# One ring of seven PSUM banks and another order of matmuls in an attention kernel

## The chip, the cores and the metric

The kernel runs on one core of one Trainium2 chip. The core's engines work side by side and are tied by semaphores: TensorE (PE in the profile, its weight loads PEld), VectorE (DVE), ScalarE (ACT), GpSimd (POOL) and SyncE (SP, which here only issues DMAs). PE writes its results to PSUM, which has eight banks of 128 partitions by 512 float32; DVE and ACT read them from there. The metric is the device time of one execution in microseconds. Before the change the median of 3 runs is 2832.03 us (2831.45 to 2834.38).

## The reference

Two attentions over the same 2048 rows of 576 are mixed by a gate. Attention A has 32 heads of 18 with their own keys and values, attention B has 32 heads of queries over one shared key and value.

```python
x = A_x
g = sigmoid((x * gate_w).sum(-1, keepdims=True))
# A: q, k, v = split(x @ wqkv) into 32 heads; B: q = x @ wq in 32 heads, k = x @ wk, v = x @ wv shared
scores = einsum("bhqd,bhkd->bhqk", q, k) * 18 ** -0.5
o = einsum("bhqk,bhkd->bhqd", softmax(scores), v)      # then heads side by side, @ wo
return g * a + (1 - g) * b
```

All is float32. The queries and the shared key of B are drawn eight times as large, so the softmax needs the maximum of each row.

## The kernel before, in words

The 64 heads of both attentions (those of B first) run one behind the other, each as 16 steps of 128 keys (or, for the maxima, 128 queries). Projections are done first; queries and keys come back from DRAM into tiles `qs` and `ks` that hold everything twice, at partitions 0 (`SB`) and 64 (`MB`). A float32 value is kept as a high and a low part, three products stacked to 54 rows; two more rows hold ones on the side of the keys and the negated row maximum on the side of the queries, so that one matmul of 56 rows gives score minus maximum.

One step T of the main loop has three parts.

- Scores (`step_scores`): four matmuls (chunks of 512 queries), each into a PSUM bank, each followed by an exp on ACT into an SBUF tile `pt` (12 of them).
- Maxima (`step_max`), 22 steps (`LEAD`) ahead of the scores: four matmuls with the queries as weights, 512 keys each. DVE reduces each bank to a column. In every second step two of the four are taken together: one matmul computes the scores for the difference of two key chunks (`kd`), ACT takes the relu of it into `xb`, and DVE adds `xb` to the other chunk's scores and takes the maximum in one custom operation. A pair of steps has eight max matmuls, seven DVE operations and nine ACT operations.
- Sums (`step_pv`): the exps times the values, with a column of ones for the denominator, added up in the bank `acc` over the 16 steps of a head. Four matmuls, one for each chunk, stand side by side in four groups of 32 columns of PE. P takes step A of the pair before over all 512 columns, h0 and h1 take step B in halves of 256.

When a head's sums are complete, `head_out` copies `acc` to `oe` on ACT and sends it off. When a head's maxima are complete, `max_rows` reduces and transposes them on DVE, splits them on POOL, and sends them through DRAM into rows 54 and 55 of `qs` (two DMAs on SP; four for the last two heads). The output projection (`out_proj`) is cut into 96 units of one PSUM tile each, 12 matmuls of 288 columns for the first 64 (`pm`, L507) and 3 for the last 32. `due` spreads them: 32 over T = 521 to 857, 32 over T = 942 to 1008, the last from T = 1021.

The order of all engines is the order in which the Python emits them (`manual_schedule`); each engine runs its instructions in that order. Two steps A and B are emitted together from one string of names: s is scores, m maxima, the digit the chunk. A matmul on `SB` and one on `MB` that follow each other run at the same time on the two halves of PE's rows. PSUM: `ps_s` three banks for scores and projections, `ps_m` four for maxima, units and the small rest, `ps_o` the accumulator. A tile takes the banks of its pool in turn, and its first matmul waits until the bank's last readers are done.

Of the kernel before, what the change touches and what calls it, by code (L numbers as in the profile page):

```python
# [17 lines left out]
S = 2048  # L18
# [24 lines left out]
def gated_mix_kernel(ctx: ExitStack, tc: tile.TileContext, xT, wall, wv, wo, out):  # L43
# [97 lines left out]

    def project(mt, c, w):

        fp = ps_s.tile([P, 512], F32, name="ps")
# [12 lines left out]
        if c == 1 and mt in HAS_K:  # L157
            d = stp.tile([P, 512], F32, name="pd", bufs=1)
            nc.vector.tensor_tensor(d, fp, KD.pop(mt), op=OP.subtract)
            dh, dl = (stp.tile([P, 512], F32R, name=f"pd{y}", bufs=1) for y in "hl")  # L160
            split(d, dh, dl, nc.scalar, nc.vector)
        dma(qk_d[0][mt * P:(mt + 1) * P, cs], h, nc.scalar)
        dma(qk_d[1][mt * P:(mt + 1) * P, cs], l, nc.gpsimd)
        if c == 1 and mt in HAS_K:
            dma(kd_d[0][mt * P:(mt + 1) * P, :], dh, nc.scalar)
            dma(kd_d[1][mt * P:(mt + 1) * P, :], dl, nc.gpsimd)
        if mt == 0:
            dma(z_d[cs], st[ROW_G:ROW_G + 1, :], nc.scalar)
            return c, st

    def shared_v(c, st):
        pv = ps_m.tile([P, 512], F32, name="pm")
# [9 lines left out]
        nc.gpsimd.memset(t, 1.0)  # L182

    def project_v(st_, hf, w):
        fp = ps_s.tile([P, 512], F32, name="ps")
        for n, (a, b, k, kr) in enumerate(PROJ):
            nc.tensor.matmul(fp[:, 0:288], X[b][:kr, k, st_ * P:(st_ + 1) * P], w[a][:kr, k, :],  # L187
                             start=(n == 0), stop=(n == len(PROJ) - 1))
# [129 lines left out]
    def kst(u):  # L318
        return ksb if u < H else L["ks"][(u - H) % 3]
# [6 lines left out]

    MX = {}

    def step_max(u, i, c):

        if i == 0 and c == 0:
            MX[u] = mxs[u] if u < 2 else mxs[2 + u % 3]
        early = 16 * u + i < LEAD
        both = not early and i % 2 == 0
        b = SB if early and c % 2 else MB
        pm = ps_m.tile([P, 512], F32, name="pm")
        k = kst(u)[b:b + 54, c * 512:(c + 1) * 512]
        if both and c < 2:  # L340
            k = L["kd", u if u >= H else 0][b:b + 54, :] if c == 0 else kst(u)[b:b + 54, 0:512]
        nc.tensor.matmul(pm, qs[u % 3][b:b + 54, i * P:(i + 1) * P], k, start=True, stop=True)  # L342
        if both and c == 0:
            MX["x"] = lead.tile([P, 512], F32, name="xb", bufs=2)
            nc.scalar.activation(MX["x"], pm, AF.Relu)  # L345
        elif both and c == 1:
            junk = lead.tile([P, 512], BF16, name="junk", bufs=1)
            nc.vector.tensor_tensor_reduce(junk, pm, MX.pop("x"), 1.0, -3e38, op0=OP.add, op1=OP.max,  # L348
                                           accum_out=MX[u][:, i, c:c + 1])
        else:  # L350
            nc.vector.tensor_reduce(MX[u][:, i, c:c + 1], pm, axis=AX.X, op=OP.max)  # L351

    def max_rows(u):


        m = ms[u % 2]
        nc.vector.tensor_reduce(m[:, 0:16], MX.pop(u), axis=AX.X, op=OP.max, negate=True)
        mt = lead.tile([P, 32], F32, name="mt")
        nc.vector.transpose(mt, m)  # L359
        mh = lead.tile([P, 2, 32], F32R, name="mh")  # L360
        split(mt, mh[:, 0, :], mh[:, 1, :], nc.gpsimd, nc.gpsimd)
        md = m_d[u % 4]
        dma(md, mh.rearrange("p a f -> p (a f)"))
        for b in (SB, MB) if u > NU - 3 else (SB,):
            for a in range(2):
                dma(qs[u % 3][b + 54 + a:b + 55 + a, :].rearrange("o (i b f) -> o i b f", b=4, f=32),
                    md.rearrange("(b i) (o a f) -> o a i b f", i=32, o=1, a=2)[:, a, 0:16])

    PT = {}

    def step_scores(u, i, c, alone):

        b = SB
        ps = (ps_m if alone and c < 2 else ps_s).tile([P, 512], F32, name="pm" if alone and c < 2 else "ps")
        if alone and c % 2:
            b = MB
        nc.tensor.matmul(ps, kst(u)[b:b + 56, i * P:(i + 1) * P],  # L377
                         qs[u % 3][b:b + 56, c * 512:(c + 1) * 512], start=True, stop=True)
        PT["q"] = PT.get("q", []) + [(c, ps)]
        if alone and c == 0:  # L380
            return
        for c, ps in PT.pop("q"):
            pt = L["pt"].tile([P, 512], F32, name="pt")
            nc.scalar.activation(pt, ps, AF.Exp, scale=SCALE)  # L384
            PT[u, i, c] = pt

    def step_pv(u, i, a, b):

# [88 lines left out]
    def out_proj(t0, rows, first=False):  # L477
# [18 lines left out]
        for q in range(8):  # L496
# [3 lines left out]
            for s2 in range(2):  # L500
                st_ = 2 * q + s2
                for hf in range(2):
                    fp = ps_m.tile([P, 512], F32, name="pm")
                    n = 0
                    for a, b in PRODS:
                        for t, r in enumerate(rows):
# [27 lines left out]
    def last_out():  # L534
# [6 lines left out]
        for j in range(4):  # L541
# [4 lines left out]
        pt = ps_m.tile([P, 512], F32, name="pm")  # L546
# [7 lines left out]
        yield  # L554
        for st_ in range(16):
            for hf in range(2):
                ps = ps_m.tile([P, 512], F32, name="pm")
# [49 lines left out]

    vunits = [(st_, hf) for hf in range(2) for st_ in range(16)]

    for T in range(-LEAD, NSTEP + 2, 2):  # L610
        if T == 0:
            open_ph2()
# [5 lines left out]
        alone = M >= NSTEP  # L618
        units = sum(due(t, Tb, Tc, 32) for t in (T, T + 1) for _, _, _, Tb, Tc in SEG)
        for op in "sA0 mA0 P sA1 mA1 sA2 mA2 sA3 mA3 h0 sB0 mB0 sB1 mB1 h1 sB2 mB2 sB3 mB3".split():  # L620
            if op[0] == "m":
                if T < 0 and op[2] == "0":
                    while len(vunits) > 32 * (-T - 1 - (op[1] == "B")) // LEAD:
                        project_v(*vunits[0], WV[vunits[0][1]])
                        vunits.pop(0)
                if not alone:
                    step_max(*divmod(M + (op[1] == "B"), 16), int(op[2]))
            elif op[0] == "s":
                if 0 <= T < NSTEP:
                    step_scores(*divmod(T + (op[1] == "B"), 16), int(op[2]), alone)  # L630
# [4 lines left out]
            if op[0] == "h" and units:  # L635
                pull(1)
                units -= 1
        pull(units)
        if slow and M % 16:
            for _ in range(2 if T > 1000 else 1):  # L640
# [45 lines left out]
```

## Time and profile before

| | |
|---|---|
| median of 3 runs | 2832.03 us |
| profiled execution | 2830.23 us, span 2828.1 us, mean granted clock 0.996 |
| PE busy | 2801.4 us (99%) |
| ACT busy | 2447.0 us (87%) |
| DVE busy | 2371.8 us (84%) |
| exps, L384 | 4052 records, 613 ns mean |
| reductions, L351 | 3094 records, 681 ns mean |
| score matmuls, L377, and max matmuls, L342 | 433 to 435 ns and 439 to 471 ns mean |
| sums, L391 | 12288 records, 457 ns mean |
| copy of the sums, L401 | 63 records, 617 ns median |

Durations overlap: the next instruction of an engine starts before the one before it has ended, so the interval between two starts is the price, not the duration. Some records of instructions are missing. PE's busy time has modelled ends. A row of the order of time has the start, the length, the engine, the line, the operation, output and input tile, the count of like instructions that were merged, and in brackets the idle time before them with what ended it.

### The profile page before, as it was taken

To read this page: it belongs to the slowest core of one execution; us is meant where nothing else is said; L and a number is where in the kernel's file an instruction comes from. 1 tells how busy PE (TensorE), PEld (TensorE's weight loads), DVE (VectorE), ACT (ScalarE), POOL (GpSimd) and SP (SyncE) were. 2 spreads that over 40 slices of the span, in tenths; PEclk is the share of its full clock that TensorE was granted. 3 is DMA by queue.
4 is the path that set the end of the run, shared out by engine and by line. 5 is a ranking of instruction groups with operands and counts; after the bars stand their busy time and mean duration, and the time that the engine had idled before them with its cause. 6 is when DMAs were issued, how large, how long until landed. Compare 5 with 4: busy or idle time off the path is not lost.

```text
span 2828.1 us, 58626 instructions
## 1 busy us (share of the span) xinstructions
PE 2801.4 (99%) x22628; PEld 1289.3 (46%) x22628; DVE 2371.8 (84%) x4461; ACT 2447.0 (87%) x4832; POOL 207.6 (7%) x364
## 2 busy tenths in 40 slices
PE   7999999999999999999999999999999999999999
PEld 5888443343433433434434444444444444345554
DVE  3346999999999999999999888888888888998765
ACT  3331999999999999999999999999999999997775
POOL 2220000011001000100110001000100011011000
PEclk9999999999999999999999999999999999999998
DMA  8662011121112111211143233233232323243412
GB/s 251 236 222 71 25 29 32 32 57 46 38 26 60 45 32 34 70 40 30 44 107 92 69 84 94 60 84 82 73 84 75 80 68 86 59 104 97 101 35 91
DMA packets 137147, 215.16 MB, mean 76 GB/s; under 512 B 55437, under 2 KB 94301, under 8 KB 125182
## 3 DMA queue, kind: packets, MB, share of 16 engines
q1 hardware_dynamic: 116156, 168.13, 22.6%
q10 hardware_dynamic: 14120, 22.30, 2.2%
q0 software_dynamic: 6592, 20.99, 2.1%
q8 instruction: 178, 2.92, 0.4%
q14 instruction: 101, 0.83, 0.1%
HBM read 137.31 MB, written 64.77 MB: 71 GB/s over the span
## 4 chain that ended last, share of the span: by engine, by line
PE 95%; DMA 2%; DVE 1%; SPq 0%; issue 0%; ACT 0%; POOL 0%; DVEq 0%; ACTq 0%; POOLq 0%
PE ps L377 40%; PE acc L391 38%; PE pm L342 6%; PE ps L147 5%; PE pm L507 4%; PE ps L187 2%; DMA xs<-xT 1%; DVE oacc L561 0%; PE pm L377 0%; DMA ksb<-qkl 0%; SPq L49 0%; DVE oacc L515 0%; DMA qkh<-ph 0%; DMA vg<-v_d 0%; DMA qkl<-pl 0%; DMA ksa<-qkh 0%
## 5 line engine op out<-in xcount | busy, mean ns | idle before, releaser
L384 ACT ACTIVATE pt<-ps 128x512 f32<-128x512 f32 x4052 | 2111.6, 613 | 106.0 <-PE pm L342 37.5
L351 DVE TENSOR_REDUCE mx<-pm 128x1 f32<-128x512 f32 x3094 | 1902.0, 681 | 63.1 <-PE pm L342 53.7
L377 PE MATMUL ps<-qs,ksb 56*128 56x512 f32 x2688 | 905.3, 433 | 0.0
L342 PE MATMUL pm<-ksb,qs 54*128 54x512 f32 x2363 | 815.3, 440 | 0.2
L377 PEld LDWEIGHTS ps<-qs,ksb 56*128 56x128 f32 x2688 | 442.8, 184 | 657.5 <-ACT pt L384 628.8
L391 PE MATMUL acc<-pt,vg 128*19 128x256 f32 (+1 forms) x6144 | 591.3, 457 | 0.8 <-ACT oe L401 0.8
L391 PE MATMUL acc<-pt,vb 128*19 128x256 f32 (+1 forms) x6144 | 591.5, 457 | 0.0
L348 DVE CUSTOM_DVE_ANT_0 junk<-pm,xb 128x512 bf16<-128x512 f32 x501 | 345.9, 690 | 192.7 <-ACT xb L345 150.2
L377 PE MATMUL ps<-qs,ksa 56*128 56x512 f32 x1364 | 459.2, 435 | 0.0
L342 PE MATMUL pm<-ksa,qs 54*128 54x512 f32 x1232 | 431.1, 439 | 0.0
L342 PEld LDWEIGHTS pm<-ksb,qs 54*128 54x128 f32 x2363 | 377.4, 184 | 5.8 <-issue 3.4
L377 PEld LDWEIGHTS ps<-qs,ksa 56*128 56x128 f32 x1364 | 220.3, 184 | 318.9 <-ACT pt L384 295.4
L345 ACT ACTIVATE xb<-pm 128x512 f32<-128x512 f32 x501 | 312.7, 624 | 0.2 <-PE pm L342 0.2
L391 PEld LDWEIGHTS acc<-pt,vg 128*19 128x19 f32 x6144 | 104.3, 97 | 223.5 <-issue 214.5
L391 PEld LDWEIGHTS acc<-pt,vb 128*19 128x19 f32 x6144 | 104.2, 96 | 212.0 <-issue 204.7
L342 PEld LDWEIGHTS pm<-ksa,qs 54*128 54x128 f32 x1232 | 197.6, 184 | 0.2
L342 PE MATMUL pm<-kdb,qs 54*128 54x512 f32 x373 | 175.5, 471 | 0.4 <-DVE mx L351 0.3
L116 POOL CAST mh<-mt 128x32 fp32r<-128x32 f32 x64 | 13.5, 211 | 1723.8 <-DVE mt L359 1723.8
L150 ACT ACTIVATE ph<-ps 128x512 fp32r<-128x512 f32 x56 | 33.5, 597 | 99.6 <-PE ps L147 88.2
L156 DVE TENSOR_TENSOR pl<-ps,ph 128x512 fp32r<-128x512 f32 x56 | 38.5, 691 | 95.8 <-ACT ph L150 63.3
L147 PE MATMUL ps<-xh,wh 128*128 128x512 f32 x280 | 75.7, 401 | 18.9 <-ACT xh L210 13.7
L147 PE MATMUL ps<-xh,wl 128*128 128x512 f32 x280 | 73.4, 392 | 0.0
(99 smaller groups left out, 1346.6 us busy)
## 6 DMA issues: line engine op xcount, KB each, us to landing
qs<-qkh SPq DMA_DIRECT2D x244, 144.0 KB
qs<-qkl SPq DMA_DIRECT2D x122, 144.0 KB
qkh<-ph ACTq DMA_DIRECT2D x56, 256.0 KB
qkl<-pl POOLq DMA_DIRECT2D x56, 256.0 KB, 3.2
ksa<-qkh SPq DMA_DIRECT2D x88, 144.0 KB
onh<-oh SPq DMA_DIRECT2D x32, 256.0 KB
onl<-ol SPq DMA_DIRECT2D x32, 256.0 KB
oih<-onh SPq DMA_DIRECT2D x16, 512.0 KB
```

Source lines behind the costliest of these rows:

```text
L147: nc.tensor.matmul(fp, w[a][:kr, k, :], X[b][:kr, k, cs], start=(n == 0), stop=(n == len(PROJ) - 1))
L150: nc.scalar.activation(h, fp, AF.Copy)
L156: nc.vector.tensor_tensor(l, fp, h.bitcast(F32), op=OP.subtract)
L187: nc.tensor.matmul(fp[:, 0:288], X[b][:kr, k, st_ * P:(st_ + 1) * P], w[a][:kr, k, :], start=(n == 0), stop=(n == len(PROJ) - 1))
L342: nc.tensor.matmul(pm, qs[u % 3][b:b + 54, i * P:(i + 1) * P], k, start=True, stop=True)
L345: nc.scalar.activation(MX["x"], pm, AF.Relu)
L348: nc.vector.tensor_tensor_reduce(junk, pm, MX.pop("x"), 1.0, -3e38, op0=OP.add, op1=OP.max, accum_out=MX[u][:, i, c:c + 1])
L351: nc.vector.tensor_reduce(MX[u][:, i, c:c + 1], pm, axis=AX.X, op=OP.max)
L377: nc.tensor.matmul(ps, kst(u)[b:b + 56, i * P:(i + 1) * P], qs[u % 3][b:b + 56, c * 512:(c + 1) * 512], start=True, stop=True)
L384: nc.scalar.activation(pt, ps, AF.Exp, scale=SCALE)
L391: nc.tensor.matmul(acc[32 * j:32 * j + 19, a:b], v_of(u, i), PT[u, i, j][:, a:b], start=(i == 0), stop=(i == 15), skip_group_check=True)
L507: nc.tensor.matmul(fp[:, 0:288], o[b][:r, t, s2 * P:(s2 + 1) * P], w[a][:r, t, 288 * hf:288 * hf + 288], start=(n == 0), stop=(n == 3 * nt ...
```

## The change

One pool `ring` of seven banks takes the place of `ps_s` and `ps_m`; every tile for scores, maxima, projections and units takes its banks in turn, in the order of emission. Four strings give the order: for the lead, for pairs without a unit, for pairs with a unit, and for the last pairs, which have no maxima. A capital M or S puts the matmul on the other half of the partitions than a small letter (maxima `SB`, scores `MB`). P stays; h and H are the halves of step B's sums; Q is step B's sums over 512 columns, and U pulls a unit. In pairs with a unit, three groups of sums become two, P and Q, and the unit stands between matmuls for scores and maxima. The combined maxima move from step A to step B (`mBx` is the difference and its relu, `mB0` the custom operation). The copy of the head's sums follows H or Q at the pair's end. The row maxima go to both halves of `qs` for every head, so four DMAs instead of two. In the last pairs each score matmul is followed by its own exp, and up to four units are pulled.

```diff
-    ps_s = ctx.enter_context(tc.tile_pool(name="ps_s", bufs=3, space=PSUM))
-    ps_m = ctx.enter_context(tc.tile_pool(name="ps_m", bufs=4, space=PSUM))
+    ring = ctx.enter_context(tc.tile_pool(name="ring", bufs=7, space=PSUM))
...
-    def step_max(u, i, c):
+    def step_max(u, i, c, low=False):
...
-        early = 16 * u + i < LEAD
-        both = not early and i % 2 == 0
-        b = SB if early and c % 2 else MB
-        pm = ps_m.tile([P, 512], F32, name="pm")
-        k = kst(u)[b:b + 54, c * 512:(c + 1) * 512]
-        if both and c < 2:
-            k = L["kd", u if u >= H else 0][b:b + 54, :] if c == 0 else kst(u)[b:b + 54, 0:512]
+        both = 16 * u + i >= LEAD and i % 2 == 1
+        b = SB if low else MB
+        if c == "x":
+            k = L["kd", u if u >= H else 0][b:b + 54, :]
+        else:
+            k = kst(u)[b:b + 54, c * 512:(c + 1) * 512]
+        pm = ring.tile([P, 512], F32, name="ps")
         nc.tensor.matmul(pm, qs[u % 3][b:b + 54, i * P:(i + 1) * P], k, start=True, stop=True)
-        if both and c == 0:
+        if c == "x":
             MX["x"] = lead.tile([P, 512], F32, name="xb", bufs=2)
             nc.scalar.activation(MX["x"], pm, AF.Relu)
-        elif both and c == 1:
+        elif both and c == 0:
...
-        for b in (SB, MB) if u > NU - 3 else (SB,):
+        for b in (SB, MB):
...
-    def step_scores(u, i, c, alone):
-        b = SB
-        ps = (ps_m if alone and c < 2 else ps_s).tile([P, 512], F32, name="pm" if alone and c < 2 else "ps")
-        if alone and c % 2:
-            b = MB
+    def step_scores(u, i, c, b):
+        ps = ring.tile([P, 512], F32, name="ps")
         nc.tensor.matmul(ps, kst(u)[b:b + 56, i * P:(i + 1) * P],
                          qs[u % 3][b:b + 56, c * 512:(c + 1) * 512], start=True, stop=True)
-        PT["q"] = PT.get("q", []) + [(c, ps)]
-        if alone and c == 0:
-            return
-        for c, ps in PT.pop("q"):
-            pt = L["pt"].tile([P, 512], F32, name="pt")
-            nc.scalar.activation(pt, ps, AF.Exp, scale=SCALE)
-            PT[u, i, c] = pt
+        pt = L["pt"].tile([P, 512], F32, name="pt")
+        nc.scalar.activation(pt, ps, AF.Exp, scale=SCALE)
+        PT[u, i, c] = pt
...
+    PLAIN = "mA0 sA0 sA1 mA1 sA2 mA2 P mA3 sA3 sB0 mB2 MB3 mBx h sB1 mB0 sB2 SB3 H"
+    UNIT = "mA0 sA0 sA1 mA1 sA2 mA2 P mA3 sA3 sB0 SB1 sB2 mB2 U MB3 mBx sB3 mB0 Q"
+    ALONE = "sA0 SA1 P U sA2 SA3 U sB0 SB1 h U sB2 SB3 H U"
+    LEADS = "V mA0 MA1 mA2 MA3 V.B mB0 MB1 mB2 MB3"
...
-        for op in "sA0 mA0 P sA1 mA1 sA2 mA2 sA3 mA3 h0 sB0 mB0 sB1 mB1 h1 sB2 mB2 sB3 mB3".split():
...
+        for op in (LEADS if T < 0 else ALONE if M >= NSTEP else UNIT if units else PLAIN).split():
+            k, second, c = op[0], op[1:2] == "B", op[2:]
+            c = int(c) if c.isdigit() else c
...
+            elif k in "mM":
+                step_max(*divmod(M + second, 16), c, k == "M")
+            elif k in "sS":
+                if T < NSTEP:
+                    step_scores(*divmod(T + second, 16), c, MB if k == "S" else SB)
+            elif k == "U":
+                pull(min(units, 1))
+                units -= min(units, 1)
             elif T >= 2:
-                step_pv(*divmod(T - (2 if op == "P" else 1), 16), *{"P": (0, 512), "h0": (0, 256), "h1": (256, 512)}[op])
-                if op == "h1" and T % 16 == 0 and T < NSTEP:
+                step_pv(*divmod(T - (2 if k == "P" else 1), 16), 256 * (k == "H"), 256 if k == "h" else 512)
+                if k in "HQ" and T % 16 == 0 and T < NSTEP:
                     head_out(T // 16 - 1)
```

More of the change, by code (lines that the diff above doesn't have):

```diff
@@ L142, in project @@
     def project(mt, c, w):
-        fp = ps_s.tile([P, 512], F32, name="ps")
+        fp = ring.tile([P, 512], F32, name="ps")
         cs = slice(c * 512, (c + 1) * 512)
@@ L171, in shared_v @@
     def shared_v(c, st):
-        pv = ps_m.tile([P, 512], F32, name="pm")
+        pv = ring.tile([P, 512], F32, name="ps")
         for j in range(4):
@@ L184, in project_v @@
     def project_v(st_, hf, w):
-        fp = ps_s.tile([P, 512], F32, name="ps")
+        fp = ring.tile([P, 512], F32, name="ps")
         for n, (a, b, k, kr) in enumerate(PROJ):
@@ L502, in out_proj @@
                 for hf in range(2):
-                    fp = ps_m.tile([P, 512], F32, name="pm")
+                    fp = ring.tile([P, 512], F32, name="ps")
                     n = 0
@@ L545, in last_out @@
             dma(stk[36:54, cs], ol[32 * j:32 * j + 18, :])
-        pt = ps_m.tile([P, 512], F32, name="pm")
+        pt = ring.tile([P, 512], F32, name="ps")
         for c in range(4):
@@ L556, in last_out @@
             for hf in range(2):
-                ps = ps_m.tile([P, 512], F32, name="pm")
+                ps = ring.tile([P, 512], F32, name="ps")
                 nc.tensor.matmul(ps[:, 0:288], stk[0:54, st_ * P:st_ * P + P],
@@ L617, in gated_mix_kernel @@
             max_rows(M // 16 - 1)
-        alone = M >= NSTEP
         units = sum(due(t, Tb, Tc, 32) for t in (T, T + 1) for _, _, _, Tb, Tc in SEG)
-        for op in "sA0 mA0 P sA1 mA1 sA2 mA2 sA3 mA3 h0 sB0 mB0 sB1 mB1 h1 sB2 mB2 sB3 mB3".split():
[L621 to L630, printed above, removed]
+        for op in (LEADS if T < 0 else ALONE if M >= NSTEP else UNIT if units else PLAIN).split():
+            k, second, c = op[0], op[1:2] == "B", op[2:]
+            c = int(c) if c.isdigit() else c
+            if k == "V":
+                while len(vunits) > 32 * (-T - 1 - (c == "B")) // LEAD:
+                    project_v(*vunits[0], WV[vunits[0][1]])
+                    vunits.pop(0)
+            elif k in "mM":
[6 more added lines that the diff above has]
+                units -= min(units, 1)
             elif T >= 2:
-                step_pv(*divmod(T - (2 if op == "P" else 1), 16), *{"P": (0, 512), "h0": (0, 256), "h1": (256, 512)}[op])
-                if op == "h1" and T % 16 == 0 and T < NSTEP:
+                step_pv(*divmod(T - (2 if k == "P" else 1), 16), 256 * (k == "H"), 256 if k == "h" else 512)
+                if k in "HQ" and T % 16 == 0 and T < NSTEP:
                     head_out(T // 16 - 1)
-            if op[0] == "h" and units:
-                pull(1)
-                units -= 1
         pull(units)
```

## The prediction

> **What bounds the kernel now.** I read the page first, then stretches of the span, then the order of time inside single pairs of steps. On the page PE is busy for 99% of the span, and the chain that ended last is PE's almost alone: scores (L377), sums (L391), maxima (L342).
>
> ```profile
> span 2828.1 us, 58626 instructions
> PE 2801.4 (99%) x22628; PEld 1289.3 (46%) x22628; DVE 2371.8 (84%) x4461; ACT 2447.0 (87%) x4832; POOL 207.6 (7%) x364
> ...
> PE 95%; DMA 2%; DVE 1%; SPq 0%; issue 0%; ACT 0%; POOL 0%; DVEq 0%; ACTq 0%; POOLq 0%
> ```
>
> A busy PE is no proof of a PE at its limit, so the stages come next. The cuts are the steps T = 2, 512, 864, 942, 1002.
>
> ```profile
> 290.25:1488.20 1197.95, 1197.58 (x10199) 479.50 (x10199) 1107.94 (x2109) 1169.14 (x2325) 75.30 (x124) 1.00 0.17 44
> 1488.20:2372.10 883.90, 883.90 (x7430) 376.61 (x7429) 770.47 (x1456) 823.83 (x1639) 51.34 (x85) 1.00 0.30 79
> 2372.10:2560.00 187.90, 187.90 (x1602) 74.98 (x1600) 173.92 (x332) 183.07 (x366) 19.74 (x27) 1.00 0.34 86
> 2560.00:2750.00 190.00, 190.00 (x1548) 98.81 (x1550) 145.00 (x273) 139.09 (x272) 7.89 (x14) 1.00 0.30 79
> 2750.00:2797.50 47.50, 46.74 (x377) 18.22 (x370) 11.48 (x22) 42.79 (x85) 0.00 (x0) 1.00 0.11 27
> ```
>
> The columns are length, then PE, PEld, DVE, ACT and POOL busy, clock, DMA share and GB/s. The first stretch is 255 pairs without units, 4.70 us each; ACT is busy 98% of it and DVE 92%. So three engines are close to one another, and a wait between any two of them can set the time. Two heads' ends, seen by the copy of the sums, give the period of eight pairs, and the rows of one plain pair show where it comes from.
>
> ```profile
> 1003.34 0.62 ACT L401 ACTIVATE oe<-acc 128x512 f32<-128x512 f32 x1
> ...
> 1040.88 0.62 ACT L401 ACTIVATE oe<-acc 128x512 f32<-128x512 f32 x1
> ...
> 1041.36 1.61 ACT L384 ACTIVATE pt<-ps 128x512 f32<-128x512 f32 x3
> ...
> 1042.79 0.67 ACT L345 ACTIVATE xb<-pm 128x512 f32<-128x512 f32 x1
> ```
>
> ```profile
> 1031.31 0.50 PE L377 MATMUL ps<-qs,ksb 56*128 56x512 f32 x1
> ...
> 1031.65 0.40 PE L377 MATMUL ps<-qs,ksb 56*128 56x512 f32 x1
> ...
> 1031.88 0.39 PE L377 MATMUL ps<-qs,ksb 56*128 56x512 f32 x1
> ...
> 1031.89 0.47 PE L342 MATMUL pm<-kdb,qs 54*128 54x512 f32 x1
> ...
> 1032.29 1.05 PE L391 MATMUL acc<-pt,vb 128*19 128x512 f32 x8
> ...
> 1033.27 0.50 PE L377 MATMUL ps<-qs,ksb 56*128 56x512 f32 x1
> ...
> 1033.85 0.39 PE L377 MATMUL ps<-qs,ksb 56*128 56x512 f32 x1
> ...
> 1033.95 0.69 DVE L348 CUSTOM_DVE_ANT_0 junk<-pm,xb 128x512 bf16<-128x512 f32 x1 [0.35 <-ACT xb L345]
> ...
> 1034.18 0.63 PE L391 MATMUL acc<-pt,vb 128*19 128x256 f32 x8
> ...
> 1034.57 3.67 DVE L351 TENSOR_REDUCE mx<-pm 128x1 f32<-128x512 f32 x6
> ...
> 1034.73 0.49 PE L377 MATMUL ps<-qs,ksb 56*128 56x512 f32 x1
> ...
> 1036.54 0.47 PE L342 MATMUL pm<-kdb,qs 54*128 54x512 f32 x1
> ...
> 1036.93 1.06 PE L391 MATMUL acc<-pt,vb 128*19 128x512 f32 x8
> ```
>
> A score matmul and a max matmul start together, one on each half of the partitions; I call the two a couple. Prices on PE: the first couple after sums takes 0.34 us (1031.31 to 1031.65, its weight load shows), the next 0.23 us, the last one before sums 0.33 us (1033.85 to 1034.18). Sums of 512 columns take 0.98 us (1032.29 to 1033.27), of 256 columns 0.56 us (1034.18 to 1034.73, rounded). A couple that had to wait shows its load again, 0.34 - 0.23 = 0.11 us. The pair before has groups of 3, 3 and 2 couples: 0.90 + 0.98 + 0.90 + 0.56 + 0.67 + 0.56 = 4.57 us, while P to P is 4.64 (1032.29 to 1036.93). The 0.07 us is the last couple before P: its kdb matmul waits for a bank of four that the third reduce after the custom operation frees (1034.57 + 0.68 + 2 x 0.60 = 1036.45), so P comes 0.40 us after it and not 0.33. The head's end adds ACT's tenth operation, the reduction of the rows' maxima adds on DVE: 37.54 us for a head (1003.34 to 1040.88), 0.42 over eight times 4.64.
>
> ACT's price: from the copy's start at 1040.88 to the end of the relu at 1043.46 are five operations, 2.58 us = 0.62 + 4 x 0.49. Nine make 4.41 us of a pair.
>
> ```profile
> 1031.84 1.57 ACT L384 ACTIVATE pt<-ps 128x512 f32<-128x512 f32 x3
> ```
>
> This exp belongs to the matmul at 1031.31: 0.53 us from a late matmul to its exp. The end of an exp frees its bank for a weight load 0.05 us later:
>
> ```profile
> 1005.72 1.17 ACT L384 ACTIVATE pt<-ps 128x512 f32<-128x512 f32 x2
> ...
> 1006.94 0.18 PEld L377 LDWEIGHTS ps<-qs,ksb 56*128 56x128 f32 x1 [0.30 <-ACT pt L384]
> ```
>
> **The change, plain pairs.** The groups stay 3, 3 and 2 with the sums P, h, H, so PE's own path stays 4.57 us. No instruction is added or taken; only banks and order change. Each bank now waits for the tile seven before it, whoever reads that. Written out for one pair, mB2 waits for sA1's exp, MB3 for mA1's reduce, mBx for sA2's exp, sB1 and mB0 for the reduces of mA2 and mA3, sB2 for sA3's exp, SB3 for sB0's. The late one is mBx: a loop runs from its load to h (0.11 + 0.33 = 0.44), through h (0.56) to sB1, to sB1's exp (0.53), through six exps sB1, sB2, SB3, sA0, sA1, sA2 (0.60 + 5 x 0.49 = 3.05), and back to mBx's load (0.05). That is 4.62 us, so 0.05 us more than PE's path and 0.02 less than now. The wait that is removed (kdb on DVE, 0.07) gives way to one on ACT (0.05). DVE's seven operations are 4.2 us and no longer in a loop with PE, so the reduction of the rows' maxima is hidden.
>
> **Head's end.** The copy of the sums now stands behind the exps of sB2 and SB3, and the next P must wait for it. From sB1's load: exp at 0.53, end of the fourth operation (sB1, sB2, SB3, copy) at 0.53 + 0.62 + 3 x 0.49 = 2.62, P at 2.67. PE alone would be there at 0.34 + 0.33 + 0.56 + 0.90 = 2.13. So P waits 0.54 us, in which mBx's 0.05 disappears: this pair takes 4.62 + 0.49 = 5.11. A head is 7 x 4.62 + 5.11 = 37.45 against 37.54, a gain of 0.09; unrounded durations give 0.13. Over the 59 heads up to T = 942: 5 to 8 us, I take 7.
>
> **Pairs with a unit.** Now the unit stands between h0 and a couple:
>
> ```profile
> 2562.25 0.63 PE L391 MATMUL acc<-pt,vg 128*19 128x256 f32 x8
> ...
> 2562.81 0.79 PE L507 MATMUL pm<-woh,oih 128*128 128x288 f32 x4
> ...
> 2564.58 0.49 PE L377 MATMUL ps<-qs,ksa 56*128 56x512 f32 x1
> ...
> 2569.19 0.79 PE L507 MATMUL pm<-woh,oih 128*128 128x288 f32 x4
> ```
>
> The unit takes 1.77 us (2562.81 to 2564.58) and unit to unit 6.38. Afterwards the pair is three couples, P, three couples, unit, two couples, Q of 512: 0.90 + 0.98 + 0.90 + 1.77 + 0.67 + 0.98 = 6.20; before by the same prices 4.57 + 1.77 = 6.34. Two sums of 256 (1.12) become one of 512 (0.98): 0.14 saved. One switch is new, couple to unit; the nearest row is the stage of the lead, where a matmul of the same full height follows two couples:
>
> ```profile
> 216.91 0.73 PE L342 MATMUL pm<-ksb,qs 54*128 54x512 f32 x4
> 217.58 0.93 PE L187 MATMUL ps<-vwh,xh 128*128 128x288 f32 x5
> ```
>
> 0.67 us for two couples and the switch is the same 0.34 + 0.33 as before sums. I price it so; 0.23 (no switch) and 0.56 (as long as a sum of 256) are the ends, 0.1 down and 0.23 up for each of 64 units, -6 and +15 us. [...]
>
> The 33 dense pairs (T = 942 to 1008) are PE's own: 32 x 0.14 = 4.5 us. The 32 single units of the first segment cost (883.90 - 22 x 37.54) / 32 = 1.81 us each now; after, 6.20 - 4.62 = 1.58, and the pair behind it gains little, since PE then runs on its path while ACT is ahead. Between 0.14 and 0.23 each I take 0.18: 6 us.
>
> **The rest.** Eleven pairs without maxima: couples replace single scores, but eight exps at 0.49 are 3.9 us and now fill the pair: 0 to 3 us, I take 1. The lead and the projections keep their order, with PE busy throughout; only banks are added: 0 to 1, I take 0. Each head gets two more loads of the row maxima, 0.6 us each on SP. What hides them is time to spare:
>
> ```profile
> 1026.89 1.23 SPq L49 DMA_DIRECT2D qs<-m_d  x2
> 1028.17 0.84 SPq L49 DMA_DIRECT2D qs<-qkh  x2
> ```
>
> Two issues take 1.23 us, so four end at about 1029.4. The queries behind them on SP come 1.2 us later. The scores that need the rows begin three pairs after the reduction at 1024.2, at about 1036. Uncovered they would cost 1.2 us a head, at most 74 us.
>
> **Sum.** -7 - 4.5 - 6 - 1 = -18.5 us. The profiled execution took 2830.2 us (span 2828.1); the median of the runs is 2832.0, 1.8 above it. On the median: 2813.5 us. A difference under 0.2% (5.7 us) can't be told from no change here.
>
> **Rivals.** A, slower: mBx's loop is longer than summed. It has six ACT operations; at 0.505 us instead of 0.49 each the loop grows by 0.08 and takes 4.70. About 440 plain pairs make that +35 us: 2849. It decides from +0.04 a pair. For it: ACT is 98% busy in the plain stretch. Against: the 0.49 is measured over a chain without a gap. Chance 0.12.
> B, faster: the loop is shorter than PE's path (a bank freed 0.05 earlier is enough), and PE's 4.57 or its 4.55 unrounded decides: 0.05 to 0.07 less for some 400 pairs, 2786 to 2794. Against: the exp's 0.53 and 0.60 are seen as such. Chance 0.15.
> C, no change: the copy waits longer, by half an ACT operation (0.25), as the sums' last matmul must end first; 62 heads x 0.25 = 15 us: 2829. For it: the copy starts right behind H. Chance 0.09.
> My own case: 0.64, by itself 2805 to 2824.
>
> **How the numbers follow.** Faster by over 0.2%: my case and B, less the edge of mine, 0.77. Within 0.2%: C and a little of mine, 0.10. Slower: A and unseen waits, 0.13. The range takes in B's upper part and C, and leaves out A: 2792 to 2830.
>
> **What would show it.** Plain pairs of 4.62 us with a wait of the kdb matmul on ACT's exp and none on DVE; the pair behind a head's copy at 5.1 us, with the sums waiting half a microsecond for the copy; unit to unit 6.20 us in the dense stretch; the loads of the rows landing before use. Wrong would be the forecast if plain pairs came out at 4.67 or more (A), at 4.57 or less (B), or if a unit between couples took clearly over 1.77 + 0.33 us.

## The result and the profile after

The changed kernel takes 2871.7 us (median, 2869.8 to 2874.3) against 2832.6 us for the kernel before on the same chip: a ratio of 1.0138, 95% interval 1.0125 to 1.0151. It is 39 us slower; forecast were 18.5 us less. Its profiled span is 2871.5 us against 2828.1, so 43.4 us are to be found.

The page of the changed kernel, its engines and its chain:

```profile
span 2871.5 us, 60281 instructions
...
PE 2810.2 (98%) x22140; PEld 1388.5 (48%) x22140; DVE 2408.6 (84%) x4461; ACT 2462.3 (86%) x4832; POOL 207.2 (7%) x364
...
PE 86%; DMA 6%; ACT 4%; DVE 1%; SPq 1%; issue 1%; ACTq 0%; POOL 0%; DVEq 0%; POOLq 0%
```

PE gave up 9 points of the chain. The stretches of the prediction, cut at the same steps (columns as there):

```profile
286.90:1510.80 1223.90, 1205.95 (x10199) 542.25 (x10196) 1126.76 (x2109) 1173.56 (x2325) 75.13 (x124) 0.99 0.17 43
1510.80:2410.70 899.90, 888.01 (x7174) 410.48 (x7172) 783.62 (x1457) 830.21 (x1640) 51.22 (x85) 0.99 0.30 78
2410.70:2606.30 195.60, 192.19 (x1600) 85.55 (x1598) 176.91 (x330) 184.40 (x366) 19.66 (x27) 0.98 0.33 83
2606.30:2789.50 183.20, 183.20 (x1300) 93.96 (x1297) 145.24 (x271) 141.08 (x270) 7.84 (x14) 1.00 0.33 84
```

Against before: the lead -3.4 us (286.90 - 290.25), the plain stretch +26.0, the stretch with single units +16.0, the plain one behind it +7.7, the dense units -6.8, the end +3.9; the sum is +43.4. In the first three stretches PE was idle for 0.4 us before; now it is for 18, 12 and 3 us, and its clock was granted at 0.98 to 0.99 on average (1.00 before). Most of that idle time, 26.1 us in 54 waits between 290 and 2600 us, is P waiting for the copy at a head's end, which the prediction has in its sum. Two other things make up the loss.

**Slow places behind the reciprocals.** Of the changed kernel, in order of time, some rows behind the reciprocal of a group's row sums (in brackets the idle time before an instruction and what ended it):

```profile
605.82 0.95 DVE L421 RECIPROCAL sm<-sm 128x128 f32<-128x128 f32 x1
...
609.79 0.60 ACT L344 ACTIVATE xb<-ps 128x512 f32<-128x512 f32 x1 [0.59 <-PE ps L341]
610.44 0.18 PEld L373 LDWEIGHTS ps<-qs,ksb 56*128 56x128 f32 x1 [0.62 <-ACT xb L344]
...
610.98 0.60 ACT L376 ACTIVATE pt<-ps 128x512 f32<-128x512 f32 x1 [0.59 <-PE ps L373]
611.63 0.28 PEld L341 LDWEIGHTS ps<-ksb,qs 54*128 54x128 f32 x1 [1.00 <-ACT pt L376]
```

sB1's load (610.44) waits for the relu of mBx, the tile just before it, and the maximum behind it waits for sB1's own exp: PE and ACT run in turn instead of side by side. The bank of a tile isn't always the one of seven tiles ago: the common pool hands out banks when the program is built. Read off the built program, the number of tiles back to the last use of the same bank, in the matmuls' order with `|` for sums, is 6 to 8 in plain pairs, but around seven of the eight reciprocals in the main loop it is

```
7 6 8 7 7 7 | 7 6 6 5 3 3 | 1 1 14 12 | 11 3 3 13 11 11 | 5 10 6 5 10 8 | 5 8 6 4
```

**Plain pairs of 4.67 us.** Of the changed kernel, away from such a place:

```profile
1023.52 1.06 PE L383 MATMUL acc<-pt,vb 128*19 128x512 f32 x8
...
1026.04 0.49 PE L373 MATMUL ps<-qs,ksb 56*128 56x512 f32 x1
...
1026.62 3.05 ACT L376 ACTIVATE pt<-ps 128x512 f32<-128x512 f32 x6
...
1028.19 1.05 PE L383 MATMUL acc<-pt,vb 128*19 128x512 f32 x8
```

P to P is 4.67 us, not 4.62, and sB1's exp starts 0.58 us behind its matmul (0.589 unrounded), not 0.53. The groups by line say what stands ahead of the exps (count, shortest, median and longest ns, first and last start). Of the kernel before:

```profile
L384 ACTq EVENT_SEMAPHORE  x58: 17/17/17, 2745.5 to 2796.2; - x58
```

and of the changed one:

```profile
L376 ACTq EVENT_SEMAPHORE  x1958: 17/17/17, 292.0 to 2838.1; - x196
```

Each of these is a wait of its own on ACT's queue ahead of an exp; I call such an exp one with a second wait. An exp waits for its matmul; it also writes a `pt` tile that an exp wrote twelve exps ago. Where its bank was last read by ACT, the matmul has waited for ACT and one wait is enough. Where it was last read by DVE, as happens in a ring that mixes both readers, the exp waits for PE and for ACT's own semaphore: 1958 of 4096 exps. That the last reader decides it is borne out by the count: where the expectations below name one for another kernel (3392, 1639, 1988 in the strict ring, 128), its trace has as many such entries.

The head's end: the copy (L393) and the P behind it, of the changed kernel:

```profile
1018.20 0.62 ACT L393 ACTIVATE oe<-acc 128x512 f32<-128x512 f32 x1
...
1056.37 0.62 ACT L393 ACTIVATE oe<-acc 128x512 f32<-128x512 f32 x1
...
1057.04 1.05 PE L383 MATMUL acc<-pt,vb 128*19 128x512 f32 x8 [0.48 <-ACT oe L393]
```

P waits 0.48 us for it. This head took 38.17 us, the one before it 37.92 (from a copy at 980.28); forecast was 37.45.

### The profile page after: what moved, and what is told of

It reads as the page before. It is cut to its first block, busy times and chain, and to the rows that moved or that the text cites. A ratio compares the mean times of both kernels' runs of the same rounds, so it can differ in the third digit from the quotient of the medians.

```text
span 2871.5 us, 60281 instructions
## 1 busy us (share of the span) xinstructions
PE 2810.2 (98%) x22140; PEld 1388.5 (48%) x22140; DVE 2408.6 (84%) x4461; ACT 2462.3 (86%) x4832; POOL 207.2 (7%) x364
## 4 chain that ended last, share of the span: by engine, by line
PE 86%; DMA 6%; ACT 4%; DVE 1%; SPq 1%; issue 1%; ACTq 0%; POOL 0%; DVEq 0%; POOLq 0%
PE acc L383 34%; PE ps L341 27%; PE ps L373 14%; PE ps L146 5%; DMA qs<-qkl 5%; PE ps L499 4%; ACT pt L376 3%; PE ps L186 2%; ACT oe L393 1%; SPq L49 1%; DMA xs<-xT 0%; DVE oacc L553 0%; ACT xb L344 0%; DMA qkh<-ph 0%; DVE oacc L507 0%
## 5 line engine op out<-in xcount | busy, mean ns | idle before, releaser
L350 DVE TENSOR_REDUCE mx<-ps 128x1 f32<-128x512 f32 x3094 | 1940.6, 683 | 240.4 <-PE ps L373 138.1
L341 PE MATMUL ps<-ksb,qs 54*128 54x512 f32 x2363 | 829.4, 446 | 4.9 <-ACT pt L376 4.6
L373 PE MATMUL ps<-qs,ksb 56*128 56x512 f32 x2688 | 826.8, 434 | 0.9
L341 PEld LDWEIGHTS ps<-ksb,qs 54*128 54x128 f32 x2363 | 379.7, 185 | 455.5 <-ACT pt L376 234.8
L373 PEld LDWEIGHTS ps<-qs,ksb 56*128 56x128 f32 x2688 | 405.2, 185 | 157.6 <-DVE mx L350 130.6
L341 PE MATMUL ps<-ksa,qs 54*128 54x512 f32 x1232 | 445.8, 446 | 1.7 <-ACT pt L376 1.7
L347 DVE CUSTOM_DVE_ANT_0 junk<-ps,xb 128x512 bf16<-128x512 f32 x501 | 341.0, 681 | 14.4 <-PE ps L373 13.6
L341 PEld LDWEIGHTS ps<-ksa,qs 54*128 54x128 f32 x1232 | 203.0, 186 | 264.5 <-DVE mx L350 120.6
L344 ACT ACTIVATE xb<-ps 128x512 f32<-128x512 f32 x501 | 303.1, 605 | 22.4 <-PE ps L341 20.8
L341 PE MATMUL ps<-kdb,qs 54*128 54x512 f32 x373 | 172.9, 464 | 0.0
```

The source lines that it names most:

```text
L373: nc.tensor.matmul(ps, kst(u)[b:b + 56, i * P:(i + 1) * P], qs[u % 3][b:b + 56, c * 512:(c + 1) * 512], start=True, stop=True)
```

## Experiments

All times are medians; "before" was run beside each and took 2831.7 to 2833.7 us.

**The ring in strict turn.** The changed kernel's pool of seven becomes seven pools of one bank:

```diff
-    ring = ctx.enter_context(tc.tile_pool(name="ring", bufs=7, space=PSUM))
+    class Ring:
+        pools = [ctx.enter_context(tc.tile_pool(name=f"ring{i}", bufs=1, space=PSUM)) for i in range(7)]
+        n = 0
+        def tile(self, *a, **k):
+            self.n += 1
+            return self.pools[self.n % 7].tile(*a, **k)
+    ring = Ring()
```

> Edit: the changed kernel, with its ring of seven banks replaced by seven pools of one bank taken strictly in turn, so that each tile always gets the bank of the tile seven before it. Nothing else differs. Bank theory (the bank of a tile is chosen when the program is built, and after each of the seven reciprocals of the row sums it falls on tiles read one to three places before): the seven slow stretches, some 35 us in all, vanish, and no weight load waits over 0.3 us for the exp or relu just before it; time 2828 to 2840 us. Rival, reciprocal theory (the reciprocal itself makes VectorE late and the order of the matmuls can't absorb that): the reciprocals are still there, so the stretches stay, 2862 to 2875 us. Under both the plain pairs stay at 4.67 to 4.68 us and the pair with a head's copy at 5.2 us.

Measured: 2844.8 us, 1.0048 of before (1.0033 to 1.0063), 26.9 less than the changed kernel and 4.8 over the range. With the reciprocals still there, the slow places are gone. The same place in both, by stretches of two us in the changed kernel,

```profile
607.50:609.50 2.00, 1.83 (x10) 0.85 (x6) 2.00 (x4) 1.63 (x4) 0.00 (x0) 1.00 0.11 33
609.50:611.50 2.00, 1.31 (x10) 0.32 (x9) 0.79 (x2) 1.12 (x2) 0.00 (x0) 0.93 0.01 4
611.50:613.50 2.00, 1.87 (x11) 0.65 (x11) 0.92 (x3) 1.03 (x3) 0.00 (x0) 0.50 0.00 0
613.50:615.50 2.00, 2.00 (x14) 0.99 (x14) 1.12 (x3) 1.01 (x3) 0.46 (x2) 0.50 0.07 16
615.50:617.50 2.00, 2.00 (x10) 0.32 (x4) 0.98 (x2) 0.70 (x2) 0.00 (x0) 0.50 0.03 4
```

and in one stretch with the strict ring:

```profile
608.00:616.00 8.00, 8.00 (x74) 3.21 (x66) 7.86 (x16) 7.58 (x16) 0.92 (x3) 1.00 0.05 13
```

DVE is busy 98% of it; in the changed kernel it is about half from 609.50 on. The bank theory stands, its price is 27 us and not 35; the reciprocal theory falls. 12 us over before remain, with plain pairs at 4.68 us.

**The old order on the changed kernel's pool.** Only the pool differs from the kernel before:

```diff
-    ps_s = ctx.enter_context(tc.tile_pool(name="ps_s", bufs=3, space=PSUM))
-    ps_m = ctx.enter_context(tc.tile_pool(name="ps_m", bufs=4, space=PSUM))
+    ring = ctx.enter_context(tc.tile_pool(name="ring", bufs=7, space=PSUM))
...
```

> Edit: the kernel before, its order untouched, with its two rings replaced by the one pool of seven banks of the changed kernel, whose banks are handed out when the program is built. Bank theory: in the built program the distance between two tiles of one bank is 6 to 8 in most places, but falls to 1 to 4 behind each of the seven reciprocals, in this order of matmuls too; so the slow stretches come back without the new order, 15 to 35 us over the old order with a strict ring (2849.4), which is 2864 to 2885 us, with weight loads waiting for the exp just before them. Rival, order theory (only the new order is sensitive to the banks): 2843 to 2853 us, no stretch slower than with the strict ring.

Measured: 2875.3 us (1.0154, 1.0136 to 1.0173), 25.9 over the strict ring in this order. The slow places belong to the pool, not to the order.

**The old order on a strict ring.** The same, with the `Ring` above.

> Edit: the kernel before, its order of matmuls untouched, with its two rings of three and four banks replaced by one strict turn of seven banks. Every tile keeps its place, and no tile has fewer banks than before. Second-wait theory (an exp whose bank was last read by VectorE carries a wait on ScalarE's own semaphore beside the one on TensorE, and starts about 0.05 us later after a late matmul): 3392 of the 4096 exps carry it here, 58 before, so the kernel gets slower though nothing else is worse: 10 to 18 us over before, 2842 to 2850 us, plain pairs about 4.68 to 4.71 us, and 0.58 to 0.59 us from a late matmul to its exp. Rival, order theory (what costs in the changed kernel's plain pairs is its new order of matmuls alone): the order is the old one, so 2827 to 2834 us and 0.53 us from matmul to exp.

Measured: 2849.4 us (1.0064, 1.0048 to 1.0081), plain pairs mostly 4.67 to 4.71. Of this run, a first score behind sums and its exp:

```profile
1026.21 0.50 PE L384 MATMUL ps<-qs,ksb 56*128 56x512 f32 x1
...
1026.80 2.56 ACT L391 ACTIVATE pt<-ps 128x512 f32<-128x512 f32 x5
```

0.59 us; before it was 0.53. Of the nearly 50 exps after a gap between 1020 and 1250 us, all start 0.53 to 0.54 us behind their matmul in the kernel before, and all but one 0.59 to 0.60 here. That fits the second wait, but the reuse distances changed as well.

**Second waits added to the kernel before** (three attempts).

```diff
+            zb = lead.tile([P, 1], F32, name="zb", bufs=12)
+            nc.gpsimd.memset(zb, 0.0)
-            nc.scalar.activation(pt, ps, AF.Exp, scale=SCALE)
+            nc.scalar.activation(pt, ps, AF.Exp, bias=zb, scale=SCALE)
```

> Edit: the kernel before; each exp takes its bias (zero) from a tile of 128x1 that GpSimd sets to zero anew for each exp, twelve such tiles in turn, so that each exp carries a second wait, on GpSimd, which is long done. Order, banks and all other work stay. Second-wait theory: all exps start about 0.05 us later after a late matmul; by the lengths of the loops in a plain pair 12 to 22 us over before, 2844 to 2855 us. Rival (a wait on something long done costs nothing): 2830 to 2836 us. Were the second wait to cost time in exps that follow one another without a gap too, ScalarE would be the bound: nine operations by 0.05 us are 0.45 us a pair, 200 us in all.

Measured: 3227.6 us, in no theory's range; it doesn't answer the question. Of this run, the group of the exps:

```profile
L386 ACT ACTIVATE pt<-ps,zb 128x512 f32<-128x512 f32 x4052 | 2451.0, 715 | 197.4 <-POOL zb L385 123.9 <-PE pm L342 50.5 <-PE ps L377 19.5
```

The mean exp takes 715 ns (613 before), and exps in a row start 0.57 us apart instead of 0.48 to 0.49. Exps with a second wait on POOL and unchanged operands don't take longer (617 ns, next run), so it is the other operand that costs the time. So the wait was put on `pt`:

```diff
+            nc.gpsimd.memset(pt[0:1, 0:1], 0.0)
             nc.scalar.activation(pt, ps, AF.Exp, scale=SCALE)
```

> Edit: the kernel before; GpSimd sets one number of each tile of exps to zero before the exp writes the whole tile, so that each exp waits on GpSimd beside TensorE. The exp's own operands are those of before (the run with a bias from a fresh tile changed them: its exps took 0.09 us longer each, whatever they waited for). Second-wait theory: an exp that follows a late matmul starts about 0.05 us later, exps in a row without a gap are not longer; 12 to 25 us over before, 2844 to 2858 us. Rival (a second wait costs nothing): 2830 to 2836 us. If the exps in a row become longer too, it is 2900 us or more, and then the second wait has a price in each exp that the changed kernel's trace doesn't show. A GpSimd that comes late with its zeros would show as waits of the exps on it.

> Edit: as the run in which GpSimd writes one number of each tile of exps ahead of the exp, and VectorE instead of GpSimd splits the rows' maxima into two parts, so that GpSimd is not held up by VectorE behind the reduction of the maxima (one pair in eight took 6.6 to 7.7 us there for that). VectorE gets about 0.4 us more a head, of some 4 it has free. Second-wait theory: plain pairs of 4.68 to 4.71 us instead of 4.64 to 4.65, and no slow pair in the plain stretches: 2848 to 2870 us, of which up to 10 may be the split and GpSimd's work for the output projection. Rival (those 0.05 us a pair came from the slow pairs around them): plain pairs of 4.65 us.

Measured: 3057.9 us and, with the split of the maxima moved from POOL to DVE, 2937.8 us; both totals missed, as exps wait for POOL itself (168 and 68 us in all; in the first run 34 pairs of the plain stretch take 6 to 8 us). The other plain pairs scatter, half of all between 4.70 and 4.87 us in the first run and between 4.68 and 4.80 in the second, so they give no price of a pair. Exps after a gap start 0.59 us behind their matmul in most cases, exps in a row still 0.48 to 0.49 us apart. The price per late exp shows, a total for it doesn't.

**One second wait moved.** On the strict ring two tiles of a plain pair exchange their banks, and with them which of the two exps has the second wait:

```diff
+                if T >= 0 and op == "sB1" and not units:    # or "sA3" with q[1], or both
+                    q = ring.pools
+                    q[0], q[2] = q[2], q[0]
                 if T < NSTEP:
                     step_scores(...)
```

(`Ring.tile` takes the first pool of the list and puts it last. Of the two tiles, one now gets a bank of five or six tiles ago and the other one of nine or eight.)

> Edit: the changed kernel with the strict ring; in plain pairs sB1 and sB2 exchange their banks, so that sB1 gets the bank that ScalarE read last (sA3's) and sB2 the one that VectorE read last (mA2's). The matmuls, their order and the number of second waits (1988 exps) are those of the strict ring: the second wait only moves from sB1's exp to sB2's, which follows another exp without a gap. Second-wait theory (sB1's exp is the one in the loop that sets the plain pair, and it starts 0.05 us late): plain pairs go from 4.68 to 4.62-4.64 us and the time to 2819 to 2832 us. Rival (the second wait is a cost of ScalarE per instruction, wherever it stands): 2842 to 2848 us, as the count stays. Rival (the 0.05 us a pair comes from somewhere else in the new order): the same 2842 to 2848 us.

> Edit: the same with another exchange: sA3 and sB0 exchange their banks in plain pairs, which moves the second wait from sA3's exp to sB0's. sA3's exp too starts after a gap (0.62 us behind its matmul), but ScalarE comes to a stop again before sB1, so it is not in the loop that sets the pair. Second-wait theory with that loop: no change, 2841 to 2847 us, plain pairs at 4.67 to 4.68. Rival (every late exp costs its 0.05 us): a gain as large as that of the exchange at sB1, 2819 to 2832 us.

> Edit: both exchanges. By the prediction's own loop with its 0.53 us from matmul to exp: the plain pair is its 4.62 us, the head's pair about 5.15, and the kernel takes 2818 to 2826 us, which is the change as it was predicted (2813.5) less what the head's copy takes more. If the loop is another one, it is no faster than the exchange at sB1 alone by more than 2 us and above 2830 us.

Measured: at sB1 2834.9 us (1.0012, 1.0003 to 1.0021), at sA3 2843.0 us (1.0035, 1.0022 to 1.0048), at both 2819.6 us (0.9960, 0.9946 to 0.9974). The plain pairs are mostly 4.64 to 4.66, 4.67 to 4.68, and 4.61 to 4.62 us. The strict ring had 2844.8. Of the run with both exchanges, a copy, sB1, its exp, the next copy and the P behind it:

```profile
1001.05 0.63 ACT L400 ACTIVATE oe<-acc 128x512 f32<-128x512 f32 x1
...
1036.56 0.50 PE L380 MATMUL ps<-qs,ksb 56*128 56x512 f32 x1
...
1037.10 1.58 ACT L383 ACTIVATE pt<-ps 128x512 f32<-128x512 f32 x3
...
1038.54 0.62 ACT L400 ACTIVATE oe<-acc 128x512 f32<-128x512 f32 x1
...
1039.21 1.05 PE L390 MATMUL acc<-pt,vb 128*19 128x512 f32 x8 [0.46 <-ACT oe L400]
```

0.54 us from matmul to exp, a head of 37.49 us. The same for sA3, of the strict ring,

```profile
1036.17 0.49 PE L381 MATMUL ps<-qs,ksb 56*128 56x512 f32 x1
...
1036.79 0.60 ACT L384 ACTIVATE pt<-ps 128x512 f32<-128x512 f32 x1
```

and with both exchanges:

```profile
1035.05 0.49 PE L380 MATMUL ps<-qs,ksb 56*128 56x512 f32 x1
...
1035.61 0.60 ACT L383 ACTIVATE pt<-ps 128x512 f32<-128x512 f32 x1
```

0.62 us becomes 0.56. Matmuls, their order and the number of second waits are those of the strict ring (one exp more or less), so the cause is neither a price that each second wait has wherever it stands nor some other cost of the new order. The other banks are no cause either: in the strict ring as in all three runs, sB1's matmul starts 0.56 us behind h's and sA3's 0.99 us behind P's, so PE waits for neither bank. What changed is the time from there to the exp. sA3 alone gives nothing, as expected. sB1 alone gives 10 us, 3 less than the least expected, and both 25, as expected: once sB1 starts in time, sA3's late exp holds the pair at about 4.65. So two late exps set the pair; the prediction and my expectation knew only of sB1's.

**The unit pairs alone**, in the kernel before:

```diff
+        if units and not alone:
+            order = order.replace("h0", "U").replace("h1", "Q")
...
```

> Edit: the kernel before with one part of the change alone: in a pair with a unit of the output projection the unit stands in the place of the first half of the sums, and the sums of the second step are one matmul of 512 columns in the place of the second half. Banks and plain pairs are those of before. Theory (the unit pairs of the change were a gain, hidden under losses elsewhere): 32 dense pairs at 6.2 instead of 6.35 us and 32 single units at 0.2 less each give 9 to 18 us: 2814 to 2824 us, faster than both kernels. Rival (the new switch from a couple to the unit costs as much as a group of sums saves, and the gain seen in the changed kernel comes of its ring): 2829 to 2836 us, dense pairs 6.33 us or more.

Measured: 2822.5 us (0.9964, 0.9953 to 0.9976). Of this run, a unit's first matmul, the next score, and the next unit:

```profile
2569.13 0.80 PE L507 MATMUL pm<-woh,oih 128*128 128x288 f32 x4
...
2570.91 0.50 PE L377 MATMUL ps<-qs,ksa 56*128 56x512 f32 x1
...
2575.34 0.81 PE L507 MATMUL pm<-woh,oih 128*128 128x288 f32 x4
```

1.78 us for the unit, 6.21 from unit to unit (6.38 in the rows of before that the prediction shows, 6.35 at the median of its dense pairs). This part of the change is a gain by itself, 10 us.

**The order alone**, on the old banks and on rings by reader.

```diff
-        pm = ring.tile([P, 512], F32, name="ps")
+        pm = ps_m.tile([P, 512], F32, name="pm")            # four banks
...
-        ps = ring.tile([P, 512], F32, name="ps")
+        ps = ps_s.tile([P, 512], F32, name="ps")            # three banks
...
```

> Edit: the changed kernel with the old banks, three for the scores and four for everything else; the order of matmuls is the new one. If the order itself is a gain or harmless: 2820 to 2850 us. By the loops with a ring of three for scores: in the group sB0 mB2 MB3 mBx only one of four is a score and in P's group the three scores in turn wait for exps still running, so PE stands at the scores: 4.9 to 5.1 us a plain pair, 2950 to 3060 us; then the new order needs the common ring, and the two parts of the change can't be had singly.

> Edit: the changed kernel with two rings by reader: four banks for what ScalarE reads (scores and the matmul against kdb), three for what VectorE reads. Nearly no exp carries a second wait (128 of 4096) and no slow stretch is due to the choice of banks, but nine tiles a pair share four banks. Second-wait theory: from a late matmul to its exp 0.53 to 0.54 us again in the new order. Rival (the 0.59 us belongs to the new order): 0.58 to 0.59 us. The time, 2845 to 2870 us under the first, tells less, as the shorter rings add waits of their own.

Measured, with one run each: 3051.8 us with plain pairs of 5.07 to 5.09, so the order doesn't fit the old banks. By reader (the kdb matmul with the scores on four banks, three for the other maxima) 2876.4 us, 6 over the range. With the second wait gone from nearly all of them, sB1's exp starts 0.53 us behind its matmul and sA3's 0.56, as with both exchanges, so the 0.59 and 0.62 don't belong to the new order. But pairs stay at 4.67 to 4.70; waits for the fewer banks may be why, which no run here singles out. Some 23 us of the total are lost ahead of the first copy (350.6 us; 327.4 in the strict ring); why, I did not follow up.

**Other orders in old and strict rings.**

> Edit: the old order with the strict ring and the unit pairs of the change, and in three couples of the plain pair the maximum stands before the score: mA0 sA0 P mA1 sA1 sA2 mA2 sA3 mA3 h0 sB0 mB0 sB1 mB1 h1 mB2 sB2 sB3 mB3. With a strict ring these swaps decide who read a score's bank last: 1639 exps have two waits instead of 3392. Second-wait theory with the loops of a pair worked out from the prices on record: the plain pair falls to 4.62 to 4.64 us, the head's pair to 4.85 to 4.9, and with the units' gain the kernel takes 2796 to 2812 us, faster than both. Rival (a swap inside a couple moves nothing, as both matmuls start together): the strict ring's 2849 less the units' 10: 2836 to 2842 us.

> Edit: the kernel before with the unit pairs of the change and its two rings, and two maxima of the plain pair moved: sA0 mA0 P mB0 sA1 mA1 sA2 mA2 sA3 h0 mA3 sB0 mB1 sB1 h1 sB2 mB2 mB3 sB3. In the kernel before, the kdb matmul before P waits for the third reduce behind the custom operation, 0.07 us a pair by the prediction. Here one more maximum stands between, so that the wait on VectorE is off the path. If that wait is worth its 0.07 us: plain pairs of 4.57 to 4.62 us, 2796 to 2812 us. Rival (ScalarE, busy 98% of the plain stretch with nine operations of 0.49 us and one late start, sets the pair, not the wait on VectorE): plain pairs stay at 4.63 to 4.65 us, 2818 to 2826 us, as with the unit pairs alone.

> Edit: the kernel before with the unit pairs of the change, and the two moved maxima (mB0 to behind P, mA3 to behind h0) in the loop's pairs from T = 0 on only; the lead keeps its old order, which the run with moved maxima had slowed by about 27 us before T = 0. Theory (the plain pair is 4.62 us with the wait on VectorE off the path, as that run's plain stretch showed): its 2839.6 less 27, 2809 to 2815 us, faster than every kernel so far. Rival (its lost time in the lead was what gave its loop the slack): 2820 to 2825 us, as with the unit pairs alone.

Measured: with swapped couples 2822.3 us (0.9969, 0.9958 to 0.9980), 10 over the range but 17 under what a swap without effect would give; plain pairs mostly 4.65 to 4.74. With moved maxima 2839.6 us (1.0029): the loop's pairs were mostly 4.61 to 4.62, but the lead lost some 29 us (by the next run), with PE idle 3 of the 50 us from 200 to 250 and a granted clock of 0.93 there; the cause of that is open. With the old order kept ahead of T = 0, 2810.3 us (0.9924, 0.9911 to 0.9938), the fastest kernel of the study. Of this run, a plain pair:

```profile
1044.11 1.05 PE L391 MATMUL acc<-pt,vb 128*19 128x512 f32 x8
...
1048.30 0.18 PEld L377 LDWEIGHTS ps<-qs,ksb 56*128 56x128 f32 x1 [0.19 <-ACT pt L384]
1048.30 0.18 PEld L342 LDWEIGHTS pm<-kdb,qs 54*128 54x128 f32 x1
...
1048.73 0.63 PE L391 MATMUL acc<-pt,vb 128*19 128x512 f32 x4
```

4.62 us, and the kdb load goes with the score's and waits for no reduce. Three banks for scores and four for maxima are enough for 4.62, if the order fits.

## Why the prediction was wrong

- "Each bank now waits for the tile seven before it, whoever reads that": the step that failed first. It took a pool of seven for a strict turn; in the built kernel the distance falls to 1 around seven reciprocals. Taking the turn strictly gives back 26.9 of the 39 us.
- "to sB1's exp (0.53)": the 0.53 us was read from a kernel where nearly all exps have one wait. In the mixed ring sB1's has two and starts at 0.59, and sA3's, which the prediction doesn't have in its loop, at 0.62 instead of 0.56; the loop of 4.62 becomes 4.67. Moving these two waits gives 25.2 us, from 2844.8 to 2819.6. (The terms of the loop as printed add up to 4.63, not 4.62; the pairs with both exchanges have 4.62.) Without either fault the change takes 2819.6 us, 6 over the forecast and within its range. The sum of both, 52 us, is what the forecast lacked, but for those 6.
- Rival A, "mBx's loop is longer than summed": its place was right (the loop by way of mBx and sB1) and so was its point of decision (+0.04 a pair; the strict ring has +0.05), its cause (six ACT operations of 0.505 us) wasn't. The price is in the first operation of the row (0.59 us behind its matmul instead of 0.53), not in each (0.48 to 0.49 us apart as before), so it is luck that its 2849 us is near the strict ring's 2844.8.
- Head's end: the pair with the copy is 5.10 to 5.11 us from h to h with both exchanges (5.15 from P to P), forecast 5.11; the wait for the copy 0.46 to 0.48, forecast 0.54. Rival C (0.25 more) did not happen. The head is 37.49 us there, forecast 37.45.
- Dense units: 6.21 from unit to unit, forecast 6.20. The new switch is 0.32 to 0.33 us, as priced. Two sums of 256 made one of 512 save the 0.14 us that the rows of before gave (from unit to unit 6.35 us at the median before, 6.21 with the unit pairs alone). Units alone gave 10.1 us, forecast 10.5.
- The row maxima's two more loads: no matmul waits for them in the changed kernel's list of waits between 290 and 2600 us, as forecast.
- The last pairs: forecast -1. With both exchanges it takes 65.9 us from the last copy (2748.9 us) to the end, 61.8 before (from 2766.3). These 4.1 us more instead of 1 less are 5 of the 6 us that are left. The largest piece is one wait, of a score for DVE's late adding up of a unit:

```profile
2775.23 0.53 PE L380 MATMUL ps<-qs,ksa 56*128 56x512 f32 x1 [2.77 <-DVE oacc L514]
```

Here too the ring makes a tile wait for a reader of another kind, and the forecast had nothing for it. The kernel before has no such wait. The changed kernel hasn't either, although its end is 3.9 us longer; that I did not take apart.
- The lead: forecast 0, measured -3.4 up to T = 2 in the changed kernel and -1.1 up to the first copy with both exchanges; not taken apart.

## What to carry to other kernels

A pool of n buffers is not a turn of n: look up in the built program which buffer each tile gets, above all where a rare instruction stands in the stream, and take the turn by hand where the order was worked out by hand. In a ring whose buffers have different readers, who read a buffer last also decided here how many waits the next reader carried (58 of 4096 exps with a second one before the change, 1958 after it); that cost nothing in a row of operations (0.48 to 0.49 us apart) and delayed the first one behind a gap by 0.05 to 0.06 us, so put such waits where the engine is already busy. And a latency taken from a trace holds for the waits it was measured with (0.53 us with one, 0.59 with two).

## What the hardware showed that was not expected

- A second wait on ACT is a queue entry of 17 ns, but an exp that has caught up with its matmul starts 0.05 to 0.06 us later for it (0.53 becomes 0.59 us in the old order's strict ring and for sB1 of the new order, 0.56 becomes 0.62 for sA3). Exps in a row keep their 0.48 to 0.49 us.
- The granted clock fell to 0.50 for about six us at a slow place (the windows from 611.50 above); PE's longest idle time there was 0.69 us, and it was busy for 3.1 of the four us ahead (1.83 and 1.31). At six of the seven slow places the clock fell (on average over 10 to 11 us to 0.69 at four of them and 0.83 at two); at the one near 883 us, with an idle time as long (0.69 us), it did not (1.00 from 880 to 890 us). What sets it is not shown here.
- An exp whose bias is a tile just written by POOL took 715 ns in the mean (613 in the kernel before) and started 0.57 us behind the one before it, 0.09 us more than without that tile. Whether the operand, its place or its newness does it was not tried.
